# Turning rows on VectorE instead of TensorE: a router's tiles and an expert layer's pages, in quarter rows

## The chip, the cores and the metric

One core of a Trainium2 chip runs the whole program. Its engines are PE (matrix products), DVE (vector), ACT (scalar functions), POOL (GpSimd, which also issues the DMAs whose addresses come from a table) and SP (which issues the other DMAs); each works through its own list of instructions in order and waits on semaphores where another engine or a DMA must be done. The metric is the time of one execution on the device in microseconds, lower being better.

## The reference

Sliding-window attention with four sink tokens feeds a dense layer, and that a mixture of eight experts of which each token takes the best one. Everything is float32.

```python
keep = is_sink | in_window                       # 4 sinks, window of 128, 32 heads of 768 x 64
a = softmax(where(keep, q @ k.T / 8, -1e9));  x = a @ v        # x: 3072 tokens x 512
h = x @ w_in;  x = (h * cos(h)) @ w_out          # 512 -> 2048 -> 512
logits = x @ w_gate + modality_bias[modality_id] # 8 experts
e_idx = argmax(logits);  gate_w = softmax(logits)[e_idx]
for e in range(8):                               # 512 -> 1024 -> 512
    mask = e_idx == e
    out[mask] = gate_w[mask] * (relu(x[mask] @ w1[e]) @ w2[e])
```

## The kernel before

Each product with a weight is made of three matmuls in a reduced-precision float format: the operands are split into a high part, which ACT rounds, and a low part, which DVE or POOL subtracts.

*First stage (0 to about 790 us).* Tokens are taken in tiles of 384. A generator `ffn_tile_gen` walks through steps (tile, f) with 16 columns blocks f: 12 matmuls `hp`, DVE and ACT make h*cos(h) in `ch`, then `g_h` and `g_l`, and two steps later 9 matmuls `y` add the block's share to the tile's output. The low half of w_out doesn't stay on chip: SP reloads `wo_l` from DRAM in every step (L721). Attention of the next tiles is woven between. When a tile's sum is complete, ACT copies it to `yt` (L778) and `route_tile` is started; it goes on by a step at a time between the FFN's steps. It turns each of the tile's three sub-tiles of 128 tokens so that the 512 columns lie across partitions: four PE transposes into PSUM (L793) and a DVE copy to `yT` (L795). Eight-column matmuls `pl` with `w_gate` (L804) give the logits. DVE takes the best expert and its weight, writes the weight into a 513th column of `yt` (L833), SP puts the 128x513 sub-tile into the DRAM scratch `y_scr` (L834), and the tokens' places in the experts' lists go into a page table, `inv`.

*Second stage (about 790 us to the end).* The experts' tokens are worked through in pages of 256 rows, 14 of them here: 12 full, and two (6 and 13) with at most half a page of rows, for which other code runs. For page T+2, DVE reads the table (`gather_rows`, L1120 and helper lines) and POOL fetches two times 128 rows of 513 (`gather_go`, L1131) into `m_yg`, while page T is computed. `prelude(T)` turns a page: eight PE transposes into the PSUM tiles `m_a` (L1143), ACT casts them to the high part (L1144), DVE subtracts for the low part (L149, a helper that records every two-operand operation). `first_product` is 96 matmuls `m_h`, `second_product` 48 matmuls `m_y`; the preludes stand between the two products, a page ahead. ACT scales the result by the gate column (L1185), POOL scatters it to the output rows (L1188). When the next page has another expert (pages 6 and 7 here), its raw weights are split into high (ACT, L1097) and low (DVE, `wi_l`) on the way. In a half page's code (`full.Else()`) the order is: products and turns `m_t` of the half, `rows_ahead` (the table for a later page), `look_ahead` and `ahead` (the prelude and the splits of the next page).

The order of the second stage is the order of the code, on each engine apart; that of the first comes from a table of steps with due times, in which the generators are woven together. A wait is put in front of an instruction where it reads or overwrites what another engine or DMA has not finished, on DMAs too.

```python
        for t in range(NQ):                          # route_tile, per sub-tile
            yt = ysb[i][t]
            pt = ps_a("yT")
            for c in range(KD):
                PE.transpose(pt[:, c * P:(c + 1) * P], yt[:, c * P:(c + 1) * P], ident)
```

Of the kernel before, what the change touches and what calls it, by code (L numbers as in the profile page):

```python
# [11 lines left out]
F32 = DT.float32  # L12
# [50 lines left out]
def kernel(  # L63
# [34 lines left out]
    YC = DM + 1  # L98
# [12 lines left out]
    y_scr = dram.tile([NT, YC], F32, name="y_scr")  # L111
# [586 lines left out]
    def ffn_tile_gen(ypool_of):  # L698
# [24 lines left out]
        for c in range(n_all + LAG):  # L723
# [28 lines left out]
            if c == n_all + LAG - 3:  # L752
                for r_ in routes:
                    for _ in r_:
                        pass
                routes.clear()
                ysb[NTILE] = [ypool_of().tile([P, YC], F32, name="yt", bufs=NQ) for _ in range(NQ)]
                for t in range(NQ):
                    SP.dma_start(out=ysb[NTILE][t][:, 0:DM], in_=yp_scr[t])
            i, f = seq[c - LAG] if c >= LAG else (0, -1)  # L760
            if f == span(i)[1] - 1:
# [6 lines left out]
                elif i == NTILE:  # L768
                    for t in range(NQ):
                        yt = ysb[i][t][:, 0:DM]  # L770
# [3 lines left out]
                else:  # L774
                    ysb[i] = []
                    for t in range(NQ):
                        yt = ypool_of().tile([P, YC], F32, name="yt", bufs=NQ)
                        ACT.activation(out=yt[:, 0:DM], in_=yps[i][t], func=AF.Copy)  # L778
# [5 lines left out]
    def route_tile(i, yp):  # L784
# [3 lines left out]
        lg = yp.tile(s3, F32, name="lg")  # L788
        for t in range(NQ):
            yt = ysb[i][t]  # L790
            pt = ps_a("yT")
            for c in range(KD):
                PE.transpose(pt[:, c * P:(c + 1) * P], yt[:, c * P:(c + 1) * P], ident)  # L793
            yT = yp.tile([P, KD, P], F32, name="yT", bufs=1)
            DVE.tensor_copy(yT.rearrange("p c x -> p (c x)"), pt)  # L795
            yield 0
            for _ in range(4 if i < NTILE - 2 else 0):
                yield 0
            pl = []

            def gate(c):
                if c == 0:
                    pl.append(ps_a("pl"))
                return PE.matmul(pl[0][:, 0:NE], yT[:, c, :], wg[:, c, :], start=c == 0, stop=c == KD - 1)  # L804
# [161 lines left out]
    SP.dma_start(out=wg, in_=w_gate.rearrange("(c p) e -> p c e", p=P))  # L966
    mb = tmpc.tile([P, 2, NE], F32, name="mb")
# [102 lines left out]
    m_yg = [[fin.tile([P, YC], F32, name=f"m_yg{i}{h}") for h in range(2)] for i in range(2)]  # L1070
# [18 lines left out]
    def load_raw(e, cond=None):  # L1089
        kw = {} if cond is None else dict(cond=cond, cond_hint=False)  # L1090
        for c in range(KD):
            SP.dma_start(out=rw1[:, c, :], in_=w1[ds(e, 1), c * P:(c + 1) * P, :].rearrange("o p f -> p (o f)"), **kw)
# [19 lines left out]
    def gather(T, col, rows=NT):  # L1112
        gather_rows(T, col)
        gather_go(T, rows)
# [13 lines left out]
    def gather_go(T, rows=NT):  # L1128
        idg = m_idg[T % 4]
# [314 lines left out]
```

## Time and profile before

| what | value |
|---|---|
| median of 3 runs | 1129.12 us (1128.71 to 1129.29) |
| the profiled execution | 1130.26 us, its span 1128.5 us |
| mean granted clock of PE | 0.993 of full speed |
| PE busy | 1085.8 us, 6432 matmuls |
| DVE, ACT, POOL busy | 700.3, 607.9, 247.3 us |

The span is the time from the first to the last recorded instruction or DMA; what lies around it is the difference to the execution's own time. Engine shares are means over all stages: the stretches of the program differ, and the table by stretch in the rows below shows how. In a timeline a row is one or several like instructions; where it says how long the engine was idle in front of it, what ended that wait stands behind the arrow. PE's matmuls overlap, so that the distance from one start to the next, not the row's duration, tells what one costs.

### The profile page before, as it was taken

The numbers are of one execution on the slowest core, as the hardware profiler recorded it, in microseconds if no ns is written. First come the engines' busy times: TensorE is split into PE (matmuls) and PEld (weight loads), VectorE is DVE, ScalarE is ACT, GpSimd is POOL, SyncE is SP. The second block draws the span as 40 slices with busy tenths as digits, with TensorE's granted clock in tenths as the row PEclk, the third lists the DMA queues.
The fourth block names the chain that finished last, engine by engine and source line by source line (L and its number), as shares of the span: only waits on it lengthen the run. The fifth ranks groups of instructions, "written<-read, shape, count | busy, mean of one in ns | idle before, by whom it ended". The sixth has DMA issues, their size and how long they took to land.

```text
span 1128.5 us, 20688 instructions
## 1 busy us (share of the span) xinstructions
PE 1085.8 (96%) x6432; PEld 917.2 (81%) x6432; DVE 700.3 (62%) x2186; ACT 607.9 (54%) x1243; POOL 247.3 (22%) x337
## 2 busy tenths in 40 slices
PE   5989999999999999999999999999999998999995
PEld 3667777788788888888888889899889997899984
DVE  6677888777977877886787674746731225522210
ACT  4879888665676666665766553334222225422221
POOL 1232233322212221222222211321112211221110
PEclk9989999999999999999999999999999999999998
DMA  6466675433332542433342132624151115111110
GB/s 152 134 187 181 199 232 147 102 83 83 89 91 68 111 89 65 101 75 82 74 107 68 56 114 73 254 64 114 47 188 58 58 40 188 39 59 40 40 41 24
DMA packets 171155, 113.38 MB, mean 100 GB/s; under 512 B 130799, under 2 KB 138991, under 8 KB 170992
## 3 DMA queue, kind: packets, MB, share of 16 engines
q1 hardware_dynamic: 166672, 97.88, 32.3%
q0 software_dynamic: 4320, 13.65, 3.7%
q8 instruction: 63, 1.03, 0.4%
q14 instruction: 100, 0.82, 0.2%
HBM read 151.06 MB, written 19.67 MB: 151 GB/s over the span
## 4 chain that ended last, share of the span: by engine, by line
PE 82%; DVE 6%; DMA 4%; ACT 3%; issue 2%; POOL 1%; SPq 0%; DVEq 0%; ACTq 0%; POOLq 0%
PE hp L137 21%; PE y L676 20%; PE m_y L137 11%; PE m_h L137 10%; PE ps L137 5%; PE po L137 5%; DMA out_dram<-m_ot,m_ids 3%; PE pl L804 1%; PE pt L589 1%; PE mh L137 1%; PE yT L793 1%; PE m_a L1143 1%; DMA cv_in<-in_moe_w_in_dram 1%; PE pt L588 1%; PE pz L626 1%
## 5 line engine op out<-in xcount | busy, mean ns | idle before, releaser
L149 POOL TENSOR_TENSOR g_l<-ch,g_h 128x384 fp32r<-128x384 f32 x128 | 133.6, 1044 | 471.6 <-ACT g_h L748 408.6
L137 PE MATMUL hp<-xT_h,wi_h 128*128 128x384 f32 x512 | 186.4, 364 | 2.2 <-DVE ch L149 2.2
L137 PE MATMUL hp<-xT_h,wi_l 128*128 128x384 f32 x512 | 175.1, 342 | 0.0
L137 PE MATMUL hp<-xT_l,wi_h 128*128 128x384 f32 x512 | 174.5, 341 | 0.0
L676 PE MATMUL y<-wo_l,g_h 128*128 128x512 f32 x384 | 155.7, 406 | 2.2 <-DMA wo_l<-wl_scr 2.2
L676 PE MATMUL y<-wo,g_h 128*128 128x512 f32 x384 | 156.9, 410 | 0.0
L676 PE MATMUL y<-wo,g_l 128*128 128x512 f32 x384 | 154.5, 402 | 0.2 <-POOL g_l L149 0.2
L738 ACT ACTIVATE ch<-ch,cols 128x384 f32<-128x384 f32 x128 | 78.7, 616 | 107.8 <-DVE ch L146 107.1
L137 PE MATMUL m_y<-wi_h,hT 128*128 128x512 f32 x416 | 132.5, 393 | 0.7 <-issue 0.5
L146 DVE SCALAR_TENSOR_TENSOR hT<-m_h,hT 128x256 fp32r<-128x256 f32 x88 | 37.4, 424 | 151.0 <-ACTq L1337 102.3
L137 PEld LDWEIGHTS hp<-xT_h,wi_h 128*128 128x128 f32 x512 | 96.9, 189 | 15.5 <-issue 4.5
L748 ACT ACTIVATE g_h<-ch 128x384 fp32r<-128x384 f32 x128 | 66.3, 520 | 69.7 <-DVE ch L149 46.2
L137 PEld LDWEIGHTS hp<-xT_l,wi_h 128*128 128x128 f32 x512 | 97.2, 190 | 4.4 <-issue 1.0
L143 DVE TENSOR_SCALAR ch<-hp 128x384 int32<-128x384 f32 x128 | 70.8, 553 | 46.6 <-PE hp L137 35.4
L137 PEld LDWEIGHTS hp<-xT_h,wi_l 128*128 128x128 f32 x512 | 96.8, 189 | 1.7 <-issue 1.4
L137 PEld LDWEIGHTS m_y<-wi_h,hT 128*128 128x128 f32 x416 | 78.1, 188 | 17.0 <-issue 0.9
L149 DVE TENSOR_TENSOR ch<-ch,hp 128x384 f32<-128x384 f32 x128 | 70.0, 547 | 29.7 <-ACT ch L738 29.2
L551 ACT ACTIVATE Pb<-Pb,mx 128x272 f32<-128x272 f32 (+1 forms) x168 | 82.8, 494 | 8.4 <-DVE mx L534 7.5
L676 PEld LDWEIGHTS y<-wo,g_l 128*128 128x128 f32 x384 | 72.3, 188 | 15.1 <-POOL g_l L149 1.0
L676 PEld LDWEIGHTS y<-wo,g_h 128*128 128x128 f32 x384 | 72.3, 188 | 13.9 <-issue 3.6
L676 PEld LDWEIGHTS y<-wo_l,g_h 128*128 128x128 f32 x384 | 72.5, 189 | 11.3 <-DMA wo_l<-wl_scr 2.5
L1154 ACT ACTIVATE hT<-m_h 128x256 fp32r<-128x256 f32 x88 | 34.0, 387 | 87.6 <-PE m_h L137 86.6
(289 smaller groups left out, 2288.8 us busy)
## 6 DMA issues: line engine op xcount, KB each, us to landing
rw<-in_moe_w_dram SPq DMA_DIRECT2D x112, 512.0 KB
wo_l<-wl_scr SPq DMA_DIRECT2D x122, 256.0 KB
cv_in<-in_moe_w_in_dram SPq DMA_DIRECT2D x16, 512.0 KB
cv_out<-in_moe_w_out_dram SPq DMA_DIRECT2D x16, 512.0 KB
y_scr<-yt SPq DMA_DIRECT2D x24, 256.5 KB
xT_h<-xg_h SPq DMA_DIRECT2D x32, 192.0 KB
xT_l<-xg_l SPq DMA_DIRECT2D x32, 192.0 KB
wl_scr<-wo_l SPq DMA_DIRECT2D x16, 256.0 KB
```

The source lines that it names most:

```text
L137: PE.matmul(o, l, r, start=start, stop=stop)
L143: e.tensor_scalar(out=o, in0=i, scalar1=s1, scalar2=s2, op0=op0, op1=op1)
L146: e.scalar_tensor_tensor(out=o, in0=i0, scalar=s, in1=i1, op0=op0, op1=op1)
L149: e.tensor_tensor(out=o, in0=a, in1=b, op=op)
L551: ACT.activation(out=Pb[t][j][:, c0:c1], in_=Pb[t][j][:, c0:c1], func=AF.Exp, scale=-1.0, bias=mx[:, i:i + 1], accum_out=sm[:, i:i + 1])
L588: PE.transpose(pt[:, j, 0:P], Pb[t][j][:, 0:P], ident)
L589: PE.transpose(pt[:, j, P:2 * P], Pb[t][j][:, SEG:W3], ident)
L626: PE.transpose(pz[0:nr, t * P:(t + 1) * P], pi_, ident)
L676: i = PE.matmul(o, l, r, start=start, stop=stop)
L738: ACT.activation(out=ch, in_=ch, func=AF.Sin, scale=TWO_PI, bias=half_pi)
L748: ACT.activation(out=gh, in_=ch, func=AF.Copy)
L1154: ACT.activation(out=hT_h[f], in_=hp, func=AF.Relu)
```

## The change

- `y_scr` no longer has the gate column: it is seen as 12288 quarter rows of 128 floats, and the gate goes to its own scratch `g_scr`, put by one small DMA per tile.
- For tiles 2 to 7 (`0 < i < NTILE - 1`) a sub-tile goes to `y_scr` at once, not at the end of the routing. Two route steps later SP reads it back into the same buffer by four DMAs per sub-tile, each to 32 partitions, in pieces of 128 floats. Two steps after that DVE turns it in one STREAM_TRANSPOSE of 128x512, which turns 32x32 blocks. The logits then use `wg_t`, the rows of `w_gate` in the order that results; it is loaded by four small DMAs at the start. Four idle steps per sub-tile fall away in these tiles. Tiles 0 and 8 are routed as before.
- For pages 2 and later POOL fetches quarter rows: eight indirect DMAs of 128 quarter rows per page (`gather_x`), for page T+3 while page T is computed, and two of 128 gates (`gather_go`) for page T+2. Their indices are made by two more DVE operations in `gather_rows` from `inv4`, which is `inv` spread fourfold over the partitions once, in `spread`, by four matmuls.
- `prelude` of these pages turns by two DVE operations into `m_xr`, reading every fourth element, in place of the PE transposes. `w1` is loaded with its rows in the order that results. Pages 0 and 1 keep the PE transposes.
- In a half page's code the table for page T+3 stands where that for T+2 stood, and the gathers behind the next page's prelude.

```diff
@@ route_tile
+        turned = 0 < i < NTILE - 1
+        def put():
+            for t in range(NQ):
+                SP.dma_start(out=y_scr[(r0 + t) * P * KB:(r0 + t + 1) * P * KB, :].rearrange("(p c) y -> p (c y)", c=KB), in_=ysb[i][t])
+        if turned:
+            put()
+            yield 0
+            yield 0
+            rows = y_scr[r0 * P * KB:(r0 + NQ) * P * KB, :].rearrange("(t c p b) y -> t b p c y", t=NQ, p=TB, b=KB)
+            for t in range(NQ):
+                for b in range(KB):
+                    SP.dma_start(out=ysb[i][t][b * TB:(b + 1) * TB].rearrange("p (c y) -> p c y", c=KB), in_=rows[t, b])
+            yield 0
+            yield 0
+        wgt = wg_t if turned else wg
         for t in range(NQ):
...
+            if turned:
+                DVE.transpose(out=yT.rearrange("p k (c j) -> p k c j", j=TB),
+                              in_=ysb[i][t].rearrange("p (c k j) -> p k c j", c=KB, j=TB))
+            else:
...
-            for _ in range(4 if i < NTILE - 2 else 0):
-                yield 0
...
-        for t in range(NQ):
-            DVE.tensor_copy(ysb[i][t][:, DM:YC], gt[:, t:t + 1])
-            SP.dma_start(out=y_scr[(r0 + t) * P:(r0 + t + 1) * P, :], in_=ysb[i][t])
+        if not turned:
+            put()
+        SP.dma_start(out=g_scr[r0 * P:(r0 + NQ) * P, :].rearrange("(t p) o -> p (t o)", p=P), in_=gt)
@@ constants
+    wg_t = const.tile([P, KD, NE], F32, name="wg_t")
+    for b in range(KB):
+        SP.dma_start(out=wg_t[b * TB:(b + 1) * TB], in_=w_gate[b * P:(b + 1) * P, :].rearrange("(c p) e -> p c e", p=TB))
@@ gather_rows, gather_x, spread
+        if T > 1:
+            id8 = m_id8[i]
+            ts(DVE, m_if.rearrange("p (h c) -> p h c", c=KB), inv4[:, ds(col, 2), :], -1.0, ALU.add, 0.0, ALU.max)
+            ts(DVE, id8, m_if, float(KB), ALU.mult, bq, ALU.add)
+    def gather_x(T):
+        yg = m_yg[T % 2]
+        if T > 1:
+            for c in range(2 * KB):
+                POOL.indirect_dma_start(out=yg[:, c * P:(c + 1) * P], out_offset=None, in_=y_scr[:, :],
+                                        in_offset=bass.IndirectOffsetOnAxis(ap=m_id8[T % 4][:, c:c + 1], axis=0),
+                                        bounds_check=NT * KB - 1, oob_is_err=False)
...
+    def spread():
+        DVE.tensor_copy(inv_r, inv[:, 0:NV])
+        for g in range(KB // 2):
+            pi = ps_a("spread")[:, 0:2 * NV].rearrange("p (c n) -> p c n", c=2)
+            for c in range(2):
+                mm(pi[:, c, :], rep_t[:, 2 * g + c, :], inv_r, True, True)
+            ACT.activation(out=inv4[:, 0:NV, 2 * g:2 * g + 2].rearrange("p n c -> p c n"), in_=pi, func=AF.Copy)
@@ prelude
+            if T < 2:
...
+            else:
+                pt = m_xr[:, 2 * g:2 * g + 2]
+                DVE.transpose(out=pt.rearrange("p k (c i) -> p k c i", i=TB),
+                              in_=yg.rearrange("p (c j k) -> p k c j", k=KD, j=TB)[:, 2 * g:2 * g + 2])
             ACT.activation(out=xh[g], in_=pt, func=AF.Copy)
             tt(DVE, xl[g], pt, xh[g].bitcast(F32), ALU.subtract)
@@ run, the half page's code
             look_ahead()
-            rows_ahead()
+            rows_ahead(0)
             ahead(after)
+            rows_ahead(2)
```

SP's list behind the end of tile 2's sum, before: the three puts stand one after the other among the loads, with a wait for the gate column from DVE. In the waits, DMAHW and DMASW with a number are the completion counters of DMAs, the others those of engines.

```order
L721 DMA wo_l<-wl_scr 128x512 [waits DMAHW5_49,PE_49]
L439 DMA kn<-in_k_dram 32x12x32 [waits DMAHW6_49]
L437 DMA qn<-in_q_dram 32x12x32 [waits DMAHW7_49]
L439 DMA kn<-in_k_dram 32x12x32 [waits DMAHW0_49]
L834 DMA y_scr<-yt 128x513 [waits DMAHW1_49,DVE_49]
L834 DMA y_scr<-yt 128x513 [waits DMAHW2_49,DVE_49]
L834 DMA y_scr<-yt 128x513 [waits DMAHW3_49,DVE_49]
L721 DMA wo_l<-wl_scr 128x512 [waits DMAHW4_49,PE_49]
```

The same place now: the puts wait for ACT's copies alone, and the readbacks `yt<-y_scr` follow with one `wo_l` load between; four of twelve are shown.

```order
L795 DMA y_scr<-yt 128x512 [waits DMAHW4_49,Activation_49]
L795 DMA y_scr<-yt 128x512 [waits Activation_49]
L795 DMA y_scr<-yt 128x512 [waits DMAHW6_49,Activation_49]
L723 DMA wo_l<-wl_scr 128x512 [waits DMAHW7_49,PE_49]
L804 DMA yt<-y_scr 32x4x128 [waits DMAHW4_49,DMAHW0_49]
L804 DMA yt<-y_scr 32x4x128 [waits DMAHW1_49]
L804 DMA yt<-y_scr 32x4x128 [waits DMAHW2_49]
L804 DMA yt<-y_scr 32x4x128 [waits DMAHW3_49]
```

What moved: the puts stand ahead of the routing, and twelve DMAs that weren't there stand between two loads of `wo_l`, the first behind a wait on the counter of a put.

DVE's list in a half page's code, before, from the table's last operations to the next expert's splits: `m_ids` are the output rows of a later page, `m_x` the low parts of the next page, `wi_l` the splits.

```order
L149 TENSOR_TENSOR m_it_8590<-m_it_8590,m_ix_8586 128x2 [waits DVE_49]
L143 TENSOR_SCALAR m_ix_8586<-m_ix_8586 128x2 [waits DVE_49]
L146 SCALAR_TENSOR_TENSOR m_ids_8598<-m_it_8590,m_ix_8586 128x2 [waits DMASW6_49,DMASW7_49,DMASW4_49,DVE_49]
L149 TENSOR_TENSOR m_x_8614<-m_a_10050,m_x_8612 128x512 [waits Activation_49]
L149 TENSOR_TENSOR m_x_8615<-m_a_10051,m_x_8613 128x512 [waits Activation_49]
L1337 COMPARE_AND_BRANCH
L149 TENSOR_TENSOR wi_l_88<-rw_8578,wi_h_78 128x512 [waits DMAHW1_49,Activation_49]
```

Now: two index operations more, and two turns in the chain in front of the splits.

```order
L151 TENSOR_TENSOR m_it_8581<-m_it_8581,m_ix_8577 128x2 [waits DVE_49]
L145 TENSOR_SCALAR m_ix_8577<-m_ix_8577 128x2 [waits DVE_49]
L148 SCALAR_TENSOR_TENSOR m_ids_8589<-m_it_8581,m_ix_8577 128x2 [waits DMASW2_49,DMASW3_49,DMASW0_49,DVE_49]
L145 ISA
L145 TENSOR_SCALAR m_if<-inv_8575 128x8
L145 TENSOR_SCALAR m_id_8563<-m_if,bq 128x8 [waits DVE_49]
L1212 STREAM_TRANSPOSE m_xr<-m_yg_8557 128x512 [waits DMASW5_49,DMASW6_49,DMASW4_49,DMASW1_49]
L151 TENSOR_TENSOR m_xT_l<-m_xr,m_xT_h 128x512 [waits Activation_49]
L1212 STREAM_TRANSPOSE m_xr<-m_yg_8557 128x512
L151 TENSOR_TENSOR m_xT_l<-m_xr,m_xT_h 128x512 [waits Activation_49]
L1413 COMPARE_AND_BRANCH
L151 TENSOR_TENSOR wi_l_89<-rw_8555,wi_h_79 128x512 [waits DMAHW5_49,Activation_49]
```

What moved: the subtractions, which stood directly behind the table's operations, now each stand behind a turn of their own and ACT's cast of it; the waits of `m_ids` are still on scatters.

## Rows read from the trace of the kernel before

**Rows 1.** The page: busy time by engine; lines on the chain, share of span
```profile
PE 1085.8 (96%) x6432; PEld 917.2 (81%) x6432; DVE 700.3 (62%) x2186; ACT 607.9 (54%) x1243; POOL 247.3 (22%) x337
...
PE hp L137 21%; PE y L676 20%; PE m_y L137 11%; PE m_h L137 10%; PE ps L137 5%; PE po L137 5%; DMA out_dram<-m_ot,m_ids 3%; PE pl L804 1%; PE pt L589 1%; PE mh L137 1%; PE yT L793 1%; PE m_a L1143 1%; DMA cv_in<-in_moe_w_in_dram 1%; PE pt L588 1%; PE pz L626 1%
```

**Rows 2.** Busy time by stretch: length, each engine (instructions), clock, DMA share, GB/s
```profile
500.00:590.00 90.00, 90.00 (x541) 76.18 (x540) 68.25 (x235) 61.94 (x126) 20.48 (x28) 1.00 0.37 86
...
830.00:940.00 110.00, 110.00 (x724) 101.18 (x723) 31.95 (x85) 30.78 (x66) 17.12 (x18) 1.00 0.20 69
940.00:980.00 40.00, 35.47 (x205) 30.08 (x204) 24.20 (x55) 22.22 (x48) 8.73 (x7) 1.00 0.43 146
```

**Rows 3.** PE in time, tile turn: start, us, line, out<-in, count
```profile
450.27 0.60 PE L793 MATMUL yT<-ident,yt 128*128 128x128 f32 x4
450.63 0.48 PE L676 MATMUL y<-wo_l,g_h 128*128 128x512 f32 x1
450.94 0.40 PE L676 MATMUL y<-wo,g_l 128*128 128x512 f32 x1
```

**Rows 4.** PE in time, between a page's two products
```profile
862.15 1.04 PE L1143 MATMUL m_a<-ident,m_yg 128*128 128x128 f32 x8
...
863.26 0.39 PE L137 MATMUL m_y<-wi_l,hT 128*128 128x512 f32 x1
863.49 0.62 PE L137 MATMUL m_y<-wi_h,hT 128*128 128x512 f32 x2
```

**Rows 5.** Groups by line and shape: busy us, mean ns, idle before
```profile
L146 DVE SCALAR_TENSOR_TENSOR cv_a<-cv_h,cv_a 128x512 int32<-128x512 int32 x32 | 22.8, 711 | 0.2
...
L795 DVE COPY yT<-yT 128x512 f32<-128x512 f32 x24 | 16.5, 688 | 7.3 <-PE yT L793 7.3
...
L146 DVE SCALAR_TENSOR_TENSOR cv_a<-cv_in,cv_a 128x512 int32<-128x512 int32 x16 | 13.3, 829 | 0.1
...
L149 DVE TENSOR_TENSOR m_x<-m_a,m_x 128x512 fp32r<-128x512 f32 x14 | 9.0, 686 | 4.1 <-ACT m_x L1144 4.0
...
L476 DVE STREAM_TRANSPOSE k_r<-kn 128x512 f32<-128x512 f32 x12 | 8.3, 690 | 0.0
...
L1144 ACT ACTIVATE m_x<-m_a 128x512 fp32r<-128x512 f32 x14 | 7.6, 596 | 5.3 <-PE m_a L1143 5.3
```

**Rows 6.** DVE in time, the half page
```profile
959.40 0.16 DVE L146 SCALAR_TENSOR_TENSOR m_ids<-m_it,m_ix 128x2 uint32<-128x2 f32 x1
959.48 1.28 DVE L149 TENSOR_TENSOR m_x<-m_a,m_x 128x512 fp32r<-128x512 f32 x2
960.68 4.90 DVE L149 TENSOR_TENSOR wi_l<-rw,wi_h 128x512 fp32r<-128x512 f32 x8
965.50 0.42 DVE L146 SCALAR_TENSOR_TENSOR hT<-m_h,hT 128x256 fp32r<-128x256 f32 x1
```

**Rows 7.** POOL in time, around the half page
```profile
940.90 1.05 POOL L1131 DMA_INDIRECT m_yg<-y_scr,m_idg  x1 [0.31 <-issue]
...
946.64 1.06 POOL L1188 DMA_INDIRECT out_dram<-m_ot,m_ids  x1 [0.65 <-DMA out_dram<-m_ot,m_ids]
963.69 2.80 POOL L1131 DMA_INDIRECT m_yg<-y_scr,m_idg  x1 [15.99 <-ACT m_ot L1185]
```

**Rows 8.** The page, DMA issues: engine, op, count, us to landing
```profile
out_dram<-m_ot,m_ids POOLq DMA_INDIRECT x26, 3.0
```

**Rows 9.** SP's waits, 220 to 790: total us, times, longest
```profile
SPq L721 <- PE y L676: 261.9, 82, 7.5
```

**Rows 10.** SP in time, one load of k
```profile
329.06 0.47 SPq L439 DMA_DIRECT2D kn<-in_k_dram  x1
```

**Rows 11.** Line L738 (one per FFN step), 320 to 590: ns, first and last
```profile
L738 ACT ACTIVATE ch<-ch,cols x48: 599/617/620, 319.7 to 587.3; 128x384 f32<-128x384 f32 x48
```

**Rows 12.** ACT in time, the start
```profile
11.50 0.66 ACT L263 ACTIVATE cv_h<-cv_in 128x512 f32<-128x512 f32 x1 [9.47 <-DMA cv_in<-in_moe_w_in_dram]
12.07 0.47 ACT L472 ACTIVATE qT<-pq 128x384 f32<-128x384 f32 x1
```

More of the change, by code (lines that the diff above doesn't have):

```diff
@@ L756, in ffn_tile_gen @@
                 routes.clear()
-                ysb[NTILE] = [ypool_of().tile([P, YC], F32, name="yt", bufs=NQ) for _ in range(NQ)]
+                ysb[NTILE] = [ypool_of().tile([P, DM], F32, name="yt", bufs=NQ) for _ in range(NQ)]
                 for t in range(NQ):
-                    SP.dma_start(out=ysb[NTILE][t][:, 0:DM], in_=yp_scr[t])
+                    SP.dma_start(out=ysb[NTILE][t], in_=yp_scr[t])
             i, f = seq[c - LAG] if c >= LAG else (0, -1)
@@ L776, in ffn_tile_gen @@
                     for t in range(NQ):
[L777 to L778 removed]
+                        yt = ypool_of().tile([P, DM], F32, name="yt", bufs=NQ)
+                        ACT.activation(out=yt, in_=yps[i][t], func=AF.Copy)
                         ysb[i].append(yt)
@@ L1069 @@
     rw2 = fin.tile([P, KE, DM], F32, name="rw2")
-    m_yg = [[fin.tile([P, YC], F32, name=f"m_yg{i}{h}") for h in range(2)] for i in range(2)]
+    m_yg = [fin.tile([P, 2 * DM], F32, name=f"m_yg{i}") for i in range(2)]
+    m_gt = [fin.tile([P, 2], F32, name=f"m_gt{i}") for i in range(2)]
+    m_xr = fin.tile([P, KD, 256], F32, name="m_xr")
+    m_if = fin.tile([P, 8], F32, name="m_if")
+    m_id8 = [fin.tile([P, 8], U32, name=f"m_id8{i}") for i in range(4)]
+    bq = fin.tile([P, 1], F32, name="bq")
+    for b in range(KB):
+        POOL.memset(bq[b * TB:(b + 1) * TB], float(b))
+    rep_t = wpool.tile([P, KB, P], F32R, name="rep", tag=f"wo{KE + 6}")
+    POOL.tensor_copy(rep_t.rearrange("p c (b i) -> p c b i", i=TB),
+                     ident.rearrange("p (c i) -> p c i", i=TB).unsqueeze(2).to_broadcast([P, KB, KB, TB]))
+    inv_r = wpool.tile([P, NV], F32R, name="inv_r", tag=f"wo{KE + 7}")
+    inv4 = fin.tile([P, NV + 2, KB], F32, name="inv4")
+    POOL.memset(inv4[:, NV:], 0.0)
     m_ix = [fin.tile([P, 2], F32, name=f"m_ix{i}") for i in range(4)]
@@ L1110, in split_w2, with gather @@
         split(w2h[f], w2l[f], rw2[:, f, :], f)
-    def gather(T, col, rows=NT):
+    def gather(T, col, rows=NT, part=2):
         gather_rows(T, col)
-        gather_go(T, rows)
+        gather_go(T, rows, part)
     def gather_rows(T, col):
@@ L1350, in run, with rows_ahead @@
         cond2 = cond2 > 0 if cond2 is not None else None
-        def rows_ahead():
-            if T + 2 < NSUP:
-                with maybe(cond2):
-                    gather_rows(T + 2, val(3, T + 2, (ET.DVE,), NV - 1))
+        cond3 = flags.get((T + 3, "valid"))
+        cond3 = cond3 > 0 if cond3 is not None else None
+        def rows_ahead(step):
+            if T + 3 < NSUP:
+                with maybe(cond3):
+                    if step < 2:
+                        gather_rows(T + 3, val(3, T + 3, (ET.DVE,), NV - 1))
+                    if step > 0:
+                        gather_x(T + 3)
         if T + 2 < NSUP:
```

65 lines of the change are left out of this document (40 added, 25 removed).

## The prediction

> **What bounds the kernel now.** I read the page's first part first: PE is busy 96% of the span, DVE 62%, POOL 22%; the list of lines on the chain that ended last names the two kinds of transposes that the change takes away, yT at 1% and m_a at 1% [rows 1]. Then the table by stage: PE is full in the FFN stretch (90.00 of 90 us) and over the expert pages (110.00 of 110), where DVE has 68 of 90 and 32 of 110; the one stretch with a hole is 940 to 980, with 35.47 of 40 [rows 2]. So a matmul taken away is time won, except around 960, where PE waits for something else. A page has 96 + 8 + 48 = 152 matmuls; 724 in 110 us make 23.1 us a page. The timelines of single places then give the prices.
>
> **PE, first stage.** The four transposes of a sub-tile's turn begin at 450.27, and the second y matmul behind them at 450.94, 0.67 us later [rows 3]; one 512-column matmul alone goes on in 0.23 (863.26 to 863.49, [rows 4]). A turn costs 0.67 - 0.23 = 0.44 us of PE. Six tiles of three sub-tiles lose theirs: 18 x 0.44 = 7.9 us. DVE is not relieved: the PSUM copy that goes takes 0.69, a block transpose of 128x512 0.69 [rows 5].
>
> **PE, expert pages.** The m_a group begins at 862.15 and the second m_y behind it at 863.26: 1.11 us, less 0.23 for one m_y, is 0.88 a page [rows 4]. Twelve pages (2 to 13) lose it. At the step from page 6 to page 7 it isn't on the path, because PE waits for DVE's splits afterwards (below). 11 x 0.88 = 9.7 us.
>
> **What the pages' new prelude costs.** Today it is two casts on ACT (0.60 each) and two subtractions on DVE (0.69 each, from PSUM). Afterwards DVE turns 0.69, ACT casts 0.60, DVE subtracts 0.69, twice, in a chain: about 4.2 us with the handing over, against 1.3 us of DVE now [rows 5]. A full page has a second product of 11 us (48 m_y at 0.23) in which to do it, and DVE is idle for 70% of these stages: cost nothing. The page before the half page has 4.9 us of splits on DVE (eight, [rows 6]) and eight index operations of 0.2 beside it: 4.2 + 4.9 + 1.6 = 10.7, just under 11; I take nothing, with up to 1 us if it overruns.
>
> **The half page (946 to 966).** Here DVE is the path: the index write to m_ids at 959.40, two subtractions at 959.48, eight splits from 960.68, and PE runs unbroken only behind the hT of 965.50 [rows 6]. The changed kernel puts in front of the splits two more index operations (0.4 us) and the turns (4.2 - 1.3 = 2.9 us): 3.3 us. Besides, the write to m_ids waits for an older scatter. Today that scatter is issued at 946.64 [rows 7]; now it stands on POOL behind eight gathers, which take the place of the one at 940.90, and two of the gate. At 1.0 and 0.31 between them, with two of the eight at 2.8 as the one beside DVE's splits at 963.69 [rows 7], it goes out near 940.9 + 10 x 1.31 + 2 x 1.8 = 957.6 and lands 3.0 us later [rows 8], at about 960.7, where DVE wants it at 959.4: 1.3 us more. Sum 4.6 us; without the wait 3.3, with slow turns up to 7.
>
> **POOL.** A page now issues 4 indirect DMAs, then 12; 12 x 1.31 = 15.7 us of a page of 22.2. The gathers run two pages ahead, so nothing waits for them in a steady page. Cost nothing; if all went at 2.8 + 0.3 a page would need 37 us and POOL would be the bound, but DVE's long splits, beside which that happened, stand in few pages.
>
> **SP and the readback.** Each of six tiles adds 12 DMAs to SP, directly behind the put, the first with a wait for the put's landing; behind them stand the tile's xT loads, the next wo_l and the next q, k and v. SP issues at 0.47 us each [rows 10]: 5.6 us, and with the put's landing 8 to 9 us in which SP issues nothing else. SP has slack: it sat 261.9 us waiting to be allowed its next wo_l [rows 9]. From the eviction, the first sub-tile's four quarters are there after about 3.0 (the scatter's landing [rows 8], the nearest row for a write to DRAM) + 4 x 0.47 + 2 to 3 (the lower end an estimate for a quarter of the scatter's bytes) = 7 to 8 us. DVE meets its first turn one to two FFN steps after the eviction; 48 steps stand in 270 us [rows 11], 5.6 us each. A wait of 0 to 3 us a tile on DVE follows, on an engine that is 75% busy [rows 2] and whose results are used two steps later. Bounds: 0 to 6 x 3 = 18 us; I take 1.5 in all, near the lower end, because most of it falls into DVE's free quarter and the two steps of lag.
>
> **Start and transition.** Four small loads of wg_t go in front of cv_in, 4 x 0.47 = 1.9 us, and ACT's first cv_h waits 9.47 us for cv_in, until 11.50 [rows 12]. But the copies of qT and kT, which stood behind it (qT at 12.07), are now ahead of it, so that scores can begin earlier. -1 to +2, taken 0.5. The spreading of the page table (four 192-column matmuls, two copies on ACT, one cast) stands on PE in the transition; four of them cost PE at most 4 x 0.23 = 0.9, plus a wait for the cast up to 1: taken 0.8. The eight gathers for page 2 take 10.5 us and land 3.0 later, less than the page of 23.1 that stands in front of their use.
>
> **Sum.** -7.9 - 9.7 + 4.6 + 1.5 + 0.5 + 0.8 = -10.2 us. The profiled execution took 1130.26 (span 1128.5 and 1.76 round it) and would take 1120.1; it stands 1.1 above the median of the runs, 1129.12, which would become 1118.9.
>
> **Rivals.**
> A. All new work is hidden: no wait on the readback, the scatter lands in time, and the half page's longer list finds cover. Then -17.6, or up to 3 less for a part of the half page: 1111.5 to 1114.5. For it: DVE's and SP's slack. Against: the half page shows no cover in its rows.
> B. The pages' turns are dear. They read every fourth element, where the k_r turn in the trace reads neighbours. The nearest row is the integer operation on every second element, 0.83 against 0.71 for one on neighbours [rows 5], a factor 1.17, which would cost 0.5 us in all. At twice the time, the half page loses 1.4 and the page before it 1.1 more (1121.4); at four times, 2.8 us a turn, the two lose 4.2 and 3.9 (1127.0), while steady pages still hide a chain of 8.4 under 11. The Trainium skill, "SBUF — State Buffer", section "Door 1: The DMA port swizzle", says that an access which crosses to a new 16-byte line pays a penalty, and here each element is such a crossing; by it the upper half of this case is right, though the row at every second element shows 1.17 only and no row steps by four.
> C. The other side: the readback decides. Place: DVE's first turn of each of the six tiles, with the next steps' ch work for PE queued behind it in order, and wo_l queued on SP behind twelve issues. Point: if PE loses more than 1.9 us a tile (the sum without its 1.5 is 11.7, over six) nothing is won. Price: the last quarter at 3.0 + 12 x 0.5 + 3.0 = 12.0 us after the eviction against two steps, 11.2, for the third sub-tile, and 8 against 5.6 for the first; 2.5 us a tile gives 15 us: 1117.4 + 15 = 1132.4. For it: the readback is a write and a read one after the other, each with a landing like the scatter's 3.0. The Trainium skill, "DMA: Bandwidth & Descriptors", section "Anatomy of one DMA", puts most of some 2 us of a DMA's fixed time into the receipt of its write, heaviest for HBM; the 3.0 agrees. Against: SP's 261.9 us of slack and the lag.
> D. The change moves the order, not the time: the routes lose idle steps and the lists of the first stage shift all along, so that what PE saves there comes back as waits for other engines, and the pages' gain is eaten by the half page and B: 1127 to 1131.
>
> **How the numbers follow.** The forecast 0.45, A 0.18, B 0.17, C 0.15, D 0.05. A difference of 0.2% (2.3 us) is about what a measurement can tell. The forecast, A and most of B (all below 1126.8) are faster: 0.77. The end of B and D are the same: 0.08. C is slower: 0.15. The forecast's own range is 1115 to 1124: the half page 3.3 to 7, the readback 0 to 4, start and transition -0.5 to 3. For 8 in 10 the range reaches down past A and up to where C begins, 1110 to 1131.
>
> **What would show it.** Right: m_a transposes on PE for the first two pages alone and only six yT copies on DVE; a steady page of 22.2 instead of 23.1 us; PE full in the FFN stretch, with each tile 1.3 us shorter; DVE waiting for a scatter in front of m_ids in the half page, and its splits some 5 us later after the last m_t turn than now. Wrong: m_xr transposes well above 0.7 us (B); DVE waiting for the readback, or PE for ch or wo_l, over 2 us a tile (C); POOL busy throughout a page, so that DVE waits for gathers; or no wait at the half page (A).

## The result, and the profile after

The changed kernel took 1141.28 us (median of 4 runs, 1140.24 to 1144.91) against 1128.91 for the kernel before, whose runs beside it lay between 1125.42 and 1129.29: a ratio of 1.0124, 95% interval 1.0106 to 1.0142. That is 12.4 us slower. 1118.9 was forecast, and the range ended at 1131.

The profiled execution took 1144.91, its span is 1143.0, 14.5 more than before; it is the longest of the four, so that the stretches below add up to some 2 us more than the medians differ by. The first lines are the page's busy time and the same stretches as [rows 2] (length, then busy time and instructions of PE, weight loads, DVE, ACT, POOL; granted clock, DMA share, GB/s).

```profile
PE 1077.4 (94%) x6268; PEld 905.5 (79%) x6268; DVE 728.5 (64%) x2211; ACT 605.6 (53%) x1241; POOL 352.0 (31%) x443
```
```profile
320.00:410.00 90.00, 85.75 (x498) 72.21 (x498) 64.67 (x221) 55.62 (x117) 20.61 (x30) 0.98 0.42 94
500.00:590.00 90.00, 88.33 (x532) 74.50 (x529) 66.33 (x229) 59.03 (x123) 21.05 (x30) 1.00 0.41 94
830.00:940.00 110.00, 106.76 (x682) 96.57 (x681) 39.40 (x109) 27.18 (x57) 69.71 (x70) 1.00 0.29 94
940.00:980.00 40.00, 28.73 (x139) 23.19 (x139) 24.08 (x55) 18.53 (x40) 17.76 (x16) 0.88 0.41 143
```

PE does 164 matmuls less and the span is longer: PE was full in the FFN stretch and over the pages [rows 1, 2], and now it has holes in both, and a larger one around 960, where the granted clock is 0.88 on average. Over the whole span the mean clock is 0.984, against 0.993. The shortfall from full speed, at half speed while it lasts, is 2 x 0.016 x 1143.0 = 37 us of the lower level (1.2 GHz) against 2 x 0.007 x 1128.5 = 16. If PE had work in all of it, the extra 21 us cost 10; part of it lies in PE's wait at the half page, so this is an upper bound.

What the change was to do is there. Tile yT, after (engine, operation, count: ns min/median/max, first and last start): 18 block transposes on DVE, and six turns of four on PE for the two tiles that are routed last (7 and 0 in the code's count, not 0 and 8). The turn of the pages is beside it.

```profile
L817 PE MATMUL yT<-ident,yt x24: 270/272/309, 764.8 to 811.2; 128*128 128x128 f32 x24
L811 DVE STREAM_TRANSPOSE yT<-yt x18: 699/702/715, 240.4 to 715.4; 128x512 f32<-128x512 f32 x18
```
```profile
L1212 DVE STREAM_TRANSPOSE m_xr<-m_yg x24: 1066/1074/1090, 852.1 to 1109.2; 128x512 f32<-128x512 f32 x24
```

A table worked out from the timeline of PE shows where the 14.5 us are: the start of the transposes called lead (the first page's own, right behind the last route), and from there the time from one page's first m_h matmul to the next one's.

| us | before | after |
|---|---|---|
| span's start to lead | 790.9 | 801.4 |
| lead to page 1's m_h | 36.0 | 37.8 |
| pages 1, 2, 3, 4, 5 | 23.7, 23.3, 23.3, 23.3, 25.6 | 22.8, 22.4, 25.1, 22.4, 22.8 |
| half page (6), page 7 | 14.3, 26.3 | 23.7, 25.5 |
| pages 8 to 12 | 23.3, 23.3, 23.3, 23.5, 23.6 | 22.4, 22.4, 22.4, 22.7, 22.7 |
| page 13's start to the end | 24.9 | 26.5 |

Up to lead the forecast was -7.9 + 1.5 + 0.5 = -5.9, and it became +10.5: a miss of 16.4. Behind it -9.7 + 4.6 + 0.8 = -4.3 was forecast, and it became +4.0: a miss of 8.3. Two entries of the table vary from execution to execution: page 5's 25.6 before is 25.1 in e6 and 23.3 in e12 below, whose pages run the same code, and the 26.5 at the end after is 24.3 to 24.6 in e1, e4, e5, e7 and e11.

**A write of 1.5 KB that holds up the queue.** SP in time, after, behind the put of a tile's gates to g_scr (start, us, line, operation):

```profile
369.96 0.39 SPq L855 DMA_DIRECT2D g_scr<-rgt  x1
370.40 0.48 SPq L439 DMA_DIRECT2D qn<-in_q_dram  x1
...
373.17 0.34 SPq L723 DMA_DIRECT2D wo_l<-wl_scr  x1
373.56 4.34 SPq L439 DMA_DIRECT2D qn<-in_q_dram  x1
377.94 0.47 SPq L441 DMA_DIRECT2D kn<-in_k_dram  x1
```

The put writes 384 gates, 4 bytes each to its own address. It is itself issued in 0.39 us, but 3.6 us later the issue of one load of q takes 4.34 in place of 0.47 [rows 10]. Stretches of 3 us behind an earlier put, issued at 270.90 (columns as above):

```profile
274.00:277.00 3.00, 3.00 (x16) 2.62 (x15) 2.55 (x13) 2.97 (x7) 0.55 (x1) 1.00 0.82 10
277.00:280.00 3.00, 3.00 (x18) 2.49 (x16) 3.00 (x13) 1.29 (x2) 0.54 (x1) 1.00 0.81 37
280.00:283.00 3.00, 1.04 (x5) 0.55 (x4) 0.43 (x2) 0.52 (x1) 1.00 (x1) 1.00 0.49 77
283.00:286.00 3.00, 2.02 (x7) 1.65 (x8) 2.83 (x6) 0.88 (x2) 1.17 (x3) 0.77 0.66 208
286.00:289.00 3.00, 3.00 (x14) 3.00 (x13) 2.86 (x8) 0.52 (x2) 0.01 (x1) 0.66 0.59 132
```

The DMA engines are 82% busy and move 10 GB/s. Then PE runs dry (1.04 of 3 us), and when it has work again its clock is at the lower level for a while: 0.77 and 0.66 are means of stretches with both levels in them. The waits that went with it, DVE's from its table of waits (us in total, times, longest), PE's from its timeline:

```profile
DVE q_r L464 <- DMA wo_l<-wl_scr: 5.1, 1, 5.1
DVE q_r L464 <- DMA vs_n<-in_v_dram: 2.7, 1, 2.7
```
```profile
283.98 0.33 PE L581 MATMUL pt<-ident,Pb 128*128 128x128 f32 x1 [2.40 <-DVE Pb L143]
...
386.41 1.22 PE L139 MATMUL ps<-kT,qT 64*128 64x272 f32 x6 [3.15 <-DVE mx L536]
```

The turn of q (`q_r`) needs its load, the rows of attention that PE waits for (Pb, mx) stand behind the turn on DVE's list, and PE stands idle until they are done: at 283.17 the turn begins, at 283.67 Pb, at 283.98 PE. The same table of DVE's waits has no row for the tiles read back (yt from y_scr): the readback cost DVE no wait.

**The half page.** DVE, POOL and PE in time:

```profile
967.40 0.17 DVE L145 TENSOR_SCALAR m_ix<-m_ix 128x2 f32<-128x2 f32 x1
973.23 0.16 DVE L148 SCALAR_TENSOR_TENSOR m_ids<-m_it,m_ix 128x2 uint32<-128x2 f32 x1 [5.65 <-DMA out_dram<-m_ot,m_ids]
...
973.73 1.07 DVE L1212 STREAM_TRANSPOSE m_xr<-m_yg 128x512 f32<-128x512 f32 x1
...
978.48 4.90 DVE L151 TENSOR_TENSOR wi_l<-rw,wi_h 128x512 fp32r<-128x512 f32 x8
```
```profile
955.83 1.04 POOL L1174 DMA_INDIRECT m_yg<-y_scr,m_id  x1 [0.85 <-DVE m_id L145]
...
969.12 1.00 POOL L1187 DMA_INDIRECT m_gt<-g_scr,m_idg  x1 [0.30 <-issue]
970.42 1.03 POOL L1258 DMA_INDIRECT out_dram<-m_ot,m_ids  x1 [0.30 <-issue]
```
```profile
978.40 0.80 PE L139 MATMUL m_h<-m_x,wi_h 128*128 128x256 f32 x2 [10.69 <-ACT wi_h L1134]
```

The wait for the scatter is there as forecast, with 5.65 us in place of 1.3: eight gathers and two of the gate stand ahead of it on POOL, and the first of them was issued at 955.83, 1.1 us behind the half page's first m_h (954.74), not 5 us ahead of it as the one at 940.90 before (946.1), because its row numbers stand on DVE behind page 5's look ahead: the turns of the prelude and eight splits. PE then stands 10.69 us, and the 0.88 of the stretch above is clock of the lower level mixed in.

**Page 3.** Its step is 25.1, not 22.4. POOL and DVE in time:

```profile
877.08 1.04 POOL L1174 DMA_INDIRECT m_yg<-y_scr,m_id  x1 [0.30 <-issue]
```
```profile
879.75 1.08 DVE L1212 STREAM_TRANSPOSE m_xr<-m_yg 128x512 f32<-128x512 f32 x1 [5.17 <-DMA m_yg<-y_scr,m_id]
```

One of the page's eight gathers stands on POOL's list behind the code of page 1 and goes out alone. DVE is ready for the turn at 874.58, 2.5 us ahead of that gather's issue, and begins 2.7 us behind it.

### The profile page after: what moved, and what is told of

Its sections match the earlier page's. It is cut to its first block, busy times and chain, and to the rows that moved or that the text cites. A ratio compares the mean times of both kernels' runs of the same rounds, so it can differ in the third digit from the quotient of the medians.

```text
span 1143.0 us, 20837 instructions
## 1 busy us (share of the span) xinstructions
PE 1077.4 (94%) x6268; PEld 905.5 (79%) x6268; DVE 728.5 (64%) x2211; ACT 605.6 (53%) x1241; POOL 352.0 (31%) x443
## 5 line engine op out<-in xcount | busy, mean ns | idle before, releaser
L1174 POOL DMA_INDIRECT m_yg<-y_scr,m_id x96 | 98.5, 1026 | 39.7 <-issue 27.4
L139 PE MATMUL ps<-kT,qT 64*128 64x272 f32 (+1 forms) x504 | 75.5, 359 | 13.9 <-ACT kT L496 8.8
L678 PEld LDWEIGHTS y<-wo,g_l 128*128 128x128 f32 x384 | 72.9, 190 | 16.4 <-issue 1.4
L139 PE MATMUL m_h<-m_x,wi_h 128*128 128x256 f32 x384 | 72.7, 291 | 11.7 <-ACT wi_h L1134 10.7
```

The costliest lines, as they stand in the source:

```text
L139: PE.matmul(o, l, r, start=start, stop=stop)
L678: i = PE.matmul(o, l, r, start=start, stop=stop)
L1174: POOL.indirect_dma_start(out=yg[:, c * P:(c + 1) * P], out_offset=None, in_=y_scr[:, :], in_offset=bass.IndirectOffsetOnAxis(ap=m_id8[T % ...
```

## The experiments

Medians are given with the lowest and highest run; ratios are to the kernel before in the same job (medians 1129.2 to 1129.8), with a 95% interval.

**e1_gate_rows** and **e7_gate_wg.** The changed kernel, with the gates turned by PE and put as three rows of 512 bytes; e7 also moves the four loads of wg_t behind the first attention tile.

```diff
+        PE.transpose(pg[0:NQ, 0:P], gt, ident)
+        gr = yp.tile([NQ, P], F32, name="rgr")
+        DVE.tensor_copy(gr, pg[0:NQ, 0:P])
-        SP.dma_start(out=g_scr[...].rearrange("(t p) o -> p (t o)", p=P), in_=gt)
+        SP.dma_start(out=g_scr[...].rearrange("(t p) o -> t (p o)", p=P), in_=gr)
```

> The changed kernel with one thing different: each tile's 384 gates are turned by one PE transpose to three rows of 128 and put into the gate scratch as three pieces of 512 bytes, where the changed kernel puts 384 pieces of 4 bytes. Theory G (the small pieces: behind each such put the loads of q, k and wo_l stand still, and the last put lands some 10 us after its issue, so that the expert pages' gathers start late): the DVE waits for q_r go, POOL's wait of 21.8 us before the first gate gather falls to about 12, the wait of 5.2 us of page 3's turn goes; 1130 to 1134 us. Theory R (SP and the queues are held up by the twelve readbacks): no change beyond 2 us, 1139 to 1142. Theory O (only the order of the first stage's lists has become worse): no change, 1139 to 1142.

> The changed kernel with the gates as three rows per tile and the loads of wg_t issued after the first attention tile; the half page as changed. If the 5 us that the first 150 us lost come from the loads in front of cv_in and from the order that they bring: 3 to 5 us under the kernel with gate rows alone (1138), 1132 to 1135. If they come from the longer list of routes: no change, 1136 to 1139.

Measured: e1 1137.97 (1133.31 to 1140.01), 1.0071 [1.0046, 1.0096]; e7 1133.35 (1130.18 to 1135.49), 1.0034 [1.002, 1.0048]. e7 came in its range; e1 did not: 1137.97 lies between the 1130 to 1134 of the first theory and the 1139 of the others. The put is worth 3.3 us in the medians and 11 in the two profiled executions (1144.91 to 1133.93), the early loads of wg_t 4.6 and 2.3 (1133.93 to 1131.64). In e1 no issue of SP takes longer than 1.54 us between 200 and 830, where in the changed kernel six take 1.6 to 4.34. POOL's first gather of gates, which reads what the last put wrote, goes out 1.8 us behind that put, not 10.7, but PE has little of it: from lead to page 1's m_h e1 takes 37.5 against 37.8. Page 3's wait, which the first theory counted in, stays (4.7 us). SP of e1, then POOL of after and of e1:

```profile
367.42 0.26 SPq L859 DMA_DIRECT2D g_scr<-rgr  x1
...
369.79 0.34 SPq L723 DMA_DIRECT2D wo_l<-wl_scr  x1
370.18 0.43 SPq L439 DMA_DIRECT2D qn<-in_q_dram  x1
```
```profile
828.53 1.03 POOL L1187 DMA_INDIRECT m_gt<-g_scr,m_idg  x1 [21.80 <-issue]
```
```profile
813.23 1.03 POOL L1191 DMA_INDIRECT m_gt<-g_scr,m_idg  x1 [14.34 <-issue]
```

**e6_before_gate_put** and **e12_before_rows_put.** The kernel before, with a put of the gates added that nothing reads: in 4-byte pieces (e6), or as three rows of 512 bytes with the turn of e1 (e12).

```diff
             SP.dma_start(out=y_scr[(r0 + t) * P:(r0 + t + 1) * P, :], in_=ysb[i][t])
+        SP.dma_start(out=g_scr[...].rearrange("(t p) o -> p (t o)", p=P), in_=gt)      # e6
```

> The kernel before with one thing added: each tile's gates are also put into a scratch that nothing reads, as 384 pieces of 4 bytes, at the place where the changed kernel puts them. Theory G (the put itself stops the queue for the loads behind it): 1133 to 1140, with waits of DVE for q_r or of PE for pt some 3 to 13 us behind a put. Rival (the put only hurts who waits for its landing): 1129 to 1130.

> The kernel before with each tile's gates also put into a scratch that nothing reads, but as three rows of 512 bytes, by one PE transpose and a copy. With 384 pieces of 4 bytes this took 1147.9. If the size of the pieces is what costs: 1129 to 1132. If it is one more put at this place that costs: 1140 to 1148.

Measured: e6 1147.9 (1143.66 to 1150.48), 1.0162 [1.0135, 1.0189]; e12 1129.15 (1126.93 to 1130.7), 0.9992 [0.9982, 1.0003]. The same 1.5 KB eight times over cost 18.7 us in 4-byte pieces, more than expected, and nothing in rows. The pair shows by itself that the small pieces cost; it does not show what they cost in the changed kernel (below, step against step). PE in e6, late in the first stage, 12 to 17 us behind the puts issued at 705.98 and 785.49:

```profile
723.55 0.80 PE L677 MATMUL y<-wo_l,g_h 128*128 128x512 f32 x1 [2.52 <-DMA wo_l<-wl_scr]
...
801.87 0.79 PE L677 MATMUL y<-wo_l,g_h 128*128 128x512 f32 x1 [3.88 <-DMA wo_l<-wl_scr]
```

Here it is a wo_l that comes late, the second one issued at 787.45, 2 us behind its put. Such a wait stands in the kernel before and in e12 too, but once, with 2.2 and 2.0 us. The matmul of 512 columns then takes 0.80 where it took 0.39 [rows 4]; the granted clock over 800 to 803 is 0.75.

**e2_pages_only** and **e3_routes_only.** One part of the change each, the 4-byte put staying: in e2 the router's tiles are turned by PE again, in e3 the pages, from two gathers of whole rows.

```diff
-        turned = 0 < i < NTILE - 1
+        turned = False                 # e2
-            if T < 2 and part != 1:
+            if part != 1:              # e3, and the same in prelude
```

> The changed kernel with all tiles of the router turned by PE as before (no readback, idle steps back), the pages' part and the put of the gates in 4-byte pieces as changed. Theory G: the waits behind the gate puts stay, PE gets 7.9 us of transposes back; 1144 to 1149. Theory R: the first stage is as before, and only the pages' part remains with its half page and late gathers; 1130 to 1136. Theory O: the old order comes back with the idle steps, as R.

> The changed kernel with all pages turned by PE from two gathers of whole rows, no spreading of the table; the router's part and the gate puts as changed. All theories of the first stage expect that stage as in the changed kernel (end some 10 us later than before). The second stage then shows what the pages' part is worth: it took 341.6 us from the first page's product to the end in the changed kernel and 337.6 before. If the loss of 9.4 us at the half page comes from the turns and the crowded POOL, it goes here and the transposes' 10 us come back: 1139 to 1143. If it came with the first stage's delay, it stays: 1149 or more.

Measured: e2 1142.71 (1140.47 to 1144.73), e3 1153.71 (1151.23 to 1154.49). Neither part alone carries the loss. The whole change is 12.4 better than e3; that it is 1.4 better than e2 is less than the runs of either spread (1140.24 to 1144.91, 1140.47 to 1144.73) and shows nothing. e2 lies in no expected range. In e3 the half page lost nothing (15.0 + 26.4 against 14.3 + 26.3), so its loss comes with the pages' part, but the 1139 to 1143 that were expected with that did not come: e3 lost elsewhere, 4.1 us of it against the changed kernel in the transition, where PE waits 4.5 us for gathered rows.

**e4_half_late**, **e5_gate_half_wg**, **e8_gathers_behind.** e4 is the changed kernel with the half page's row numbers behind its splits. e5 adds to that the edits of e7. e8 is e5 with a full page's gathers behind its second scatter.

```diff
+            ahead(after)
             rows_ahead(0)
-            ahead(after)
             rows_ahead(2)
```

> The changed kernel with the table operations for page T+3 in a half page's code moved behind the next page's turn and splits on every engine's list. Theory H (DVE's 5.65 us wait for a scatter in front of m_ids holds up the turns and splits behind it; PE waits 10.7 us and its clock falls after that): PE's wait at the half page falls to 4 to 5 us; 1133 to 1136. Rival (the turns themselves, 1.07 us each with their casts, set the wait): it falls by under 2 us; 1139 to 1141.

> Three edits on the changed kernel: gates put as three rows of 512 bytes per tile; the half page's table operations behind the next page's turn and splits; the four loads of wg_t issued after the first attention tile, not in front of cv_in. If the three costs found so far (gate puts 8 us of the first stage, m_ids wait 3.6, start 5) are separate and add up: 1125 to 1131. If half of the half page's loss comes back elsewhere, as its run on the changed kernel suggests: 1131 to 1135.

> As the three edits together, and in a full page POOL issues the eight gathers for page T+3 behind the second scatter of page T instead of ahead of it. If the scatters' delay by the gathers is what m_ids waits for, and the rest of the half page's loss hangs on it: 2 to 4 us under the three edits, 1122 to 1128. If that wait is gone already: as the three edits, within 1 us.

Measured: e4 1144.23 (1141.06 to 1147.41), no gain, while the wait at the half page fell as meant. PE, e4:

```profile
975.71 0.51 PE L139 MATMUL m_h<-m_x,wi_h 128*128 128x256 f32 x2 [3.21 <-ACT wi_h L1134]
...
983.29 0.64 PE L139 MATMUL m_h<-m_x,wi_h 128*128 128x256 f32 x2 [2.31 <-DVE hT L148]
```

10.69 us became 3.21 + 2.31, and the half page with page 7 takes 16.6 + 28.8 = 45.4 instead of 49.2, but the total didn't follow and lies in no expected range: in e4's profile page 1 begins 3.9 us later behind lead than in the changed kernel's, and why isn't shown. In e5, with the put in rows, the gain shows in the time: e5 1129.08 (1126.72 to 1135.33), 1.0003 [0.9987, 1.0018], 4.3 below e7, and the half page with page 7 takes 16.3 + 27.4 = 43.7 instead of 49.2. e8 1131.58 (1128.23 to 1134.41) wins nothing over e5, and neither expectation holds: without the gathers ahead of the scatter the half page with page 7 takes 46.5 and not 43.7, so POOL's order wasn't what remained.

**e9_three_no_turn** and **e10_three_no_pages.** e5 without the router's part (the edit of e2), and e5 without the pages' part (the edit of e3).

> The three edits (gate rows, half page, late wg_t; 1129.1) without the router's part: all tiles turned by PE, no readback, idle steps back. Prediction's view (a turn costs PE 7.9 us in all and the readback little): 1134 to 1138. Accounting of the first stage's PE time in the kernel with late wg_t (6.2 us of transposes saved from 253 us on, 2.9 us more waits, 3 us more in the router's other matmuls): 1128 to 1131. Theory R (readback and its order cost more than they save): below 1128.

> The three edits (1129.1) without the pages' part: all pages turned by PE from two gathers of whole rows, gates gathered apart. If the pages' part is worth its 0.9 us a page less the half page's remaining 4 and page 3's 3: 1131 to 1134. If the gates' own gathers cost nothing and the pages' part is worth nothing: 1128 to 1130.

Measured: e9 1137.09 (1133.2 to 1140.1), e10 1141.45 (1139.0 to 1143.89), against 1129.08 for e5. Against e5, taking out the router's part costs 8.0 us and taking out the pages' part 12.4. That is not yet what the parts gain over the kernel before: 8.0 + 12.4 = 20.4, and e5 stands level with it. e9, which keeps the pages' part and all three repairs, is 7.3 us above the kernel before (some of it is lost ahead of any route, below; the rest isn't shown). A steady page takes 23.4 us in e10 and 22.4 in e5. e10, with only the router's part, lies in no expected range, 11.6 above the kernel before: from lead to the end it takes 347.7, against 337.6 before and 335.1 in e5, 4.1 of it at the half page and the rest in small pieces. The pages' part is worth so much also because without it the new frame (gates gathered apart, another order of gathers) costs by itself; how that divides wasn't tried.

**e11_three_page3.** e5 with all gathers of page 3 ahead of page 1's code.

```diff
-        gather_x(3)                    # in the transition, where only PE's order is kept as written
...
     ctx.enter_context(tc.manual_schedule())
+    gather_x(3)
```

> The three edits (1129.1) with the gathers for page 3 all in front of page 1's code on POOL; in the changed kernel one or two of the eight stand behind it, a page late, and DVE's turn of page 3 waits 4.8 us for them. If that is the cause of the long step from page 3 to 4 (24.6 to 25.9 us where others take 22.4): that step falls to 22.4 to 23, and the time to 1125 to 1127. If the step is long for another reason: 1128 to 1130.

Measured: 1127.05 (1123.59 to 1132.51), 0.9982 [0.9967, 0.9998], the fastest version, 2.8 us below the kernel before in the medians, with an interval that ends just short of 1. Page 3's step falls from 25.9 in e5 to 22.4, and DVE's turn, without a wait, follows the row ahead of it:

```profile
861.96 0.42 DVE L148 SCALAR_TENSOR_TENSOR hT<-m_h,hT 128x256 fp32r<-128x256 f32 x1 [1.01 <-ACT hT L1228]
862.30 1.07 DVE L1216 STREAM_TRANSPOSE m_xr<-m_yg 128x512 f32<-128x512 f32 x1
```

**The first stage, step against step.** ACT's `ch` operation runs once in each of the 128 FFN steps, the same in every kernel. The 21st stands ahead of any route and any put, the last some 2 us behind lead. Before, after, e1, e7 and e9, in this order (count, ns, first and last start):

```profile
L738 ACT ACTIVATE ch<-ch,cols x108: 599/617/621, 207.5 to 792.6; 128x384 f32<-128x384 f32 x108
L740 ACT ACTIVATE ch<-ch,cols x108: 598/617/627, 213.1 to 803.0; 128x384 f32<-128x384 f32 x108
L740 ACT ACTIVATE ch<-ch,cols x108: 599/617/621, 210.3 to 795.2; 128x384 f32<-128x384 f32 x108
L740 ACT ACTIVATE ch<-ch,cols x108: 600/617/622, 210.3 to 792.9; 128x384 f32<-128x384 f32 x108
L740 ACT ACTIVATE ch<-ch,cols x108: 598/617/620, 210.4 to 797.5; 128x384 f32<-128x384 f32 x108
```

| router's tiles turned by | gates put in | 21st to last step, us |
|---|---|---|
| PE | the 513th column (before) | 585.1 |
| PE | rows of 512 bytes (e12, e9) | 588.1, 587.1 |
| PE | 4-byte pieces (e6, e2) | 597.2, 592.1 |
| DVE | rows of 512 bytes (e1; e7, e5, e8, e10, e11) | 584.9; 582.6 to 582.9 |
| DVE | 4-byte pieces (after, e3, e4) | 589.9, 593.3, 595.1 |

In this stretch the 4-byte put costs 5 to 10 us in the changed kernel (against e1) and 9 in the kernel before (e6 against e12). The router's part gains 2.5 us against the kernel before and 4.4 to 5.5 against e9 and e12. The five kernels with the put in rows and late loads of wg_t agree within 0.3 us, although they reach lead between 789.4 and 798.1: what parts them is there at the 21st step already. For e5 and e11, which are furthest apart, it is mostly the clock, here from 60 to 100 and from 100 to 130 us, in e5, then in e11 (columns as above):

```profile
60.00:100.00 40.00, 36.95 (x196) 26.95 (x196) 29.17 (x75) 30.52 (x68) 10.77 (x20) 0.91 0.66 196
100.00:130.00 30.00, 27.94 (x161) 21.08 (x160) 24.81 (x56) 25.01 (x52) 7.91 (x14) 0.89 0.61 175
```
```profile
60.00:100.00 40.00, 36.78 (x215) 26.98 (x216) 29.45 (x75) 32.92 (x77) 12.27 (x28) 1.00 0.74 216
100.00:130.00 30.00, 26.78 (x170) 20.90 (x170) 26.63 (x63) 25.77 (x51) 9.02 (x15) 1.00 0.62 183
```

The code up to there is the same. If PE had work throughout, the clock takes 0.09 x 40 + 0.11 x 30 = 6.9 of the 8.5 us by which e5 is later at the 21st step. The other executions were granted between 0.89 and 1.00 there, the kernel before 0.91 and 1.00, the changed one 1.00 and 0.89, so that these two lost about the same, 3.6 and 3.3 us.

Something else is lost ahead of the 21st step, and in every kernel with the change's parts in it: after and e1 to e5 and e7 to e11 are 0.9 to 9.4 us later there than the kernel before, and PE's waits up to it add up to 21.5 to 24.7 us. In the kernel before and in e6 and e12, which have nothing of the change but a put, they are 19.5 to 21.0. It comes with wg_t early or late and with the router's part or without (e2, e9); which edit brings it isn't shown.

## Why the prediction was wrong, step by step

The forecast was 22.4 us too low. Four of its steps failed. In the list of new DMAs the put of the gates stood at nothing, and it cost 5 to 10 us of the first stage. There, too, "a matmul taken away is time won" did not hold: 2.5 us came of the 6.4. The start was put at 0.5 us, and was 5. At the half page the wait for the scatter was put at 1.3 us, and was 5.65.

- **First stage, -7.9.** The price was right, the gain was not. Between the 21st step and lead PE's yT transposes go from 8.0 us before to 1.1 in e7, as counted. But "a matmul taken away is time won" fails here: in e7 the pl, ps and pi matmuls of the same stretch take 3.8 us more, and PE waits 2.9 us more in all, 4.7 of it for Pb, which it didn't wait for before. With the readback -7.9 + 1.5 = -6.4 was forecast, and step against step it became -2.5 against the kernel before. That is rival D's mechanism, in part. The 8.0 between e9 and e5 is near 7.9 by luck: it is a distance to a kernel with a loss of its own.
- **Expert pages, -9.7.** Right: the steady step went from 23.3 to 22.4, as forecast; of the 2.8 at page 5 all but 0.5 is a step that varies with the execution (25.6 before, 23.3 in e12).
- **SP and the readback, +1.5.** Right in what it priced, and here the forecast fails. It counted "12 DMAs to SP" a tile at 0.47 each and bounded the wait of the readback; DVE had none. The thirteenth it left out. Taking the gate out of the row of 513 made one more DMA a tile, of 1.5 KB, and of its 384 separate addresses nothing was priced. No row of the trace before shows such a write, so its cost had to be bounded from both sides; the diff shows that it writes one element to a row, and I didn't list it. Its cost: 18.7 us in the kernel before (e6 against e12); in the changed one 3.3 by the medians and 5 to 10 of the first stage step against step. The Trainium skill, "DMA: Bandwidth & Descriptors", section "Specifications", says that below 512 bytes a transfer falls under line rate and becomes a read, a change and a write. e6 and e12 agree that small pieces are dear, 384 of 4 bytes against three of 512; that a read and a change are the reason no run here shows. The forecast should have weighed that rule.
- **Start, +0.5.** Wrong in size. Ahead of any route the changed kernel is 5.7 us late, and PE has waited 23.3 us where it waited 19.5 before. I read it as wg_t's four loads, which were priced at SP's issue time, and e1 to e7 gives 4.6 us by the medians, 2.3 by the profiles. But at the 21st step e1 and e7 are 2.9 and 2.8 us late, alike; 2.2 us part them only behind it. e1's two executions at a clock of 0.989 and above took 1133.3 and 1133.9, its three at 0.985 and below 1138.0 to 1140.0, so that a part of the 4.6 may be the clock. The cause of the late start stays open.
- **The miss of 16.4 up to lead.** In these two profiles 5.2 of it is there at the 21st step (5.7 us late, 0.5 forecast). The other 11.2 come behind it: 5.0 go with the put (589.9 to e1's 584.9), 2.2 with wg_t's place (to e7's 582.6), and 4.0 are what the router's part didn't gain.
- **Half page, +4.6.** Mechanism right, size wrong: 49.2 against 40.6, and the 0.88 not saved, is 9.5. Counted from the half page's first m_h, the scatter was dated 11.5 us (957.6) and went out at 15.7 (970.42): I took the gathers' place from before, though their numbers come from DVE later. The turns take 1.07, not 0.69, which adds 0.8. Rival B's turns are dearer than the unit-step turn by a factor of 1.07 / 0.70 = 1.53; in steady pages it is hidden, as forecast. The Trainium skill, "SBUF — State Buffer", section "Door 1: The DMA port swizzle", has a penalty for each access that crosses to a new 16-byte line; the 1.53 agrees in direction.
- **Page 3, no term.** 2.7 us: only page 2's gathers were dated ("10.5 us and land 3.0 later"), in one piece; one of page 3's eight stood elsewhere in POOL's list. e11 cures it.
- **Transition and tail.** +1.8 against 0.8, and 1.6 for the end, not forecast. So the miss behind lead adds up: 4.9 (half page) + 2.7 + 1.0 + 1.6 - 1.9 (page 5) = 8.3. The 1.6 and the 1.9 vary from execution to execution.
- **POOL.** Right: 69.71 us busy in 110, and no steady page waits.
- **Rivals.** A fell with the half page. C alone forecast a slower kernel (1132.4), and its mechanism was refuted: no wait for the readback at all. What it had right is that a new DMA on SP's queue delays the loads behind it, and with them PE.

In medians, the way from 1141.28 goes down by 3.3 (the put in rows), 4.6 (late wg_t), 4.3 (the half page's order) and 2.0 (page 3) to 1127.05. The last 8 us down to 1118.9 no edit won. In e11's profile, its fastest run (1123.59 where 1120.1 was forecast for the profiled execution), lead comes 1.5 us earlier than before, where 5.9 were forecast, and the time behind lead is 5.5 shorter, where 4.3 were forecast: what that run lacks it lacks in the first stage. The rest is its distance to e11's median.

Open: by what means 4-byte pieces hold up the loads behind them (the runs show only that they do); why other matmuls and waits grow when the turns go; what makes the start late, and what else e9 and e10 lose against the kernel before; and what sends an execution to the lower clock more often. e5's twelve runs go with their clock: at 0.990 and above 1126.7 to 1131.2, at 0.984 to 0.986 1133.2 to 1135.3.

## What to carry to other kernels

For each new or changed DMA, count the separate addresses, not the bytes: a column that used to ride in a wider row becomes hundreds of tiny writes when it gets a tensor of its own, and turning it into rows first costs PE and DVE next to nothing. When a queue carries loads that a full engine needs, price a DMA by how long the next loads on that queue are held up. And before dating a moved DMA by its old place, look up which instruction makes its addresses and where that one now stands in its engine's list. To price a part of a change from traces, compare the time between the same two steps: executions that reached the next stage 8.7 us apart took the same time, within 0.3 us, from the 21st step to the last.

## What the runs showed of the hardware

Eight writes of 384 pieces of 4 bytes cost 18.7 us in the kernel before, while the same bytes in three rows of 512 cost nothing that can be measured. A block transpose on DVE of 128x512 that reads every fourth element takes 1.07 us, with neighbours 0.70. An indirect DMA is issued in 1.0 us with 0.30 between two, for rows of 4 or of 512 bytes alike, and up to 1.5 beside DVE's long splits (957.17 to 960.80, after). Behind PE's wait of 2.40 us at 283.98 the clock was granted at the lower level for 2 x (0.23 + 0.34) x 3 = 3.4 us, from the two stretches at 0.77 and 0.66. One code, e5's and e11's up to the first route, was granted 0.91 and 0.89 from 60 to 130 us in one execution and 1.00 in the other.
